# Windowed attention, a two-axis Fourier mix and an FFN on one core: pieces for GpSimd, a work order without the shared-port clock, and attention scores as 64x64 products by parity of the head

## The chip, the core and the metric

The kernel runs on one core of a Trainium2 chip. A core has TensorE (PE in the profile; its weight loads are PEld), VectorE (DVE), ScalarE (ACT), GpSimd (POOL) and SyncE (SP), which here issues nearly all DMAs. Each engine works through its own queue in order, and they meet only at semaphores. The metric is the device time of one execution in microseconds (us), lower is better.

## The reference

Inputs are q, k, v of shape (8, 8, 576, 64) (batch, heads, positions, head size) and two FFN weights, 512x2048 and 2048x512, which reach the kernel as 64-bit floats.

```
scores = q @ k.T / 8, kept where 0 <= row - col < 64, softmax over col
attn   = softmax @ v                     -> x (8, 576, 512), heads side by side
X      = real(fft over positions(fft over features (x)))
u      = x + X
un     = (u - mean) / sqrt(var + 1e-6)
out    = u + relu(un @ w_ch1) @ w_ch2
```

## The kernel before

The 8 x 576 positions of all batches form 36 tiles T of 128 positions; two batches (a pair) fill 9 tiles. Because the window is 64 wide, a block of 64 queries needs only its own 64 keys and the 64 before them.

**Two ways through a tile.** Tiles T < PRO = 13 are "whole": they stay in float32. q and k are turned on TensorE (`flip`, L464), copied out of PSUM, multiplied, masked and maximized on VectorE (`masked`, L587), exponentiated on ScalarE (`expo`, L595), turned again on TensorE (`flip_p`, L606), copied, and multiplied with v (`av`, L657). Tiles from 13 on are "split": each value becomes a high and a low float16 part. The low parts (`k_lo` L484, `q_part` L495, `p_lo` L620, `u_lo` L1045, `y_lo`) are subtractions on GpSimd or VectorE, and the turns are DMA transposes issued by SP (`k_turn` L487, `q_turn` L499, `p_turn` L626, `y_turn` L765, `u_turn` L1050).

**Scores.** jj counts the two blocks of 64 queries in a tile. One PSUM bank and one `pr` buffer hold block jj, with two heads on the two halves of the partitions. In a whole tile `q_copy` writes q block-diagonally into `qbd32` (the rest was set to zero once, L370), by two copies of 64 partitions, so one 128x128 product (L568) gives two heads; four such products make one block. In a split tile (L575) the two heads go to the two column halves of the array.

**After the attention.** `radix4` (L691) does the first butterflies of the feature transform into y, y is turned and kept as yT, and when a batch is complete `fft` does the rest (folds L804 and L806, sums L830 to L858, products L890 and L924). `norm_tile` gathers the mixed rows, adds, normalizes (`rs` on GpSimd, L1022; `scale`, L1026) and turns the result into `uhl`, the FFN's input, 256 positions at a time. `ffn(c)` runs 16 steps of a first product (`ph`, L1207), a relu into two parts (`hh`, ScalarE L1222 and VectorE L1225) and a second product (`po`, L1188), in three float16 passes; the first of the 18 chunks is float32 (PLAIN = 1). The weights arrive in 32 blocks of 512 KB (`weight_piece`), and VectorE makes float32 of each in three steps (L1099, L1104, L1111) into `w0s`, `w1s` and, for the last block of the first weight, `wf`.

**The order.** Every step is an operation of the planner `Plan` with an engine (or two to choose from), a duration, a priority and its buffers. `Plan.order` simulates the engines and writes each engine's queue in the order that the simulation finds. FFN products have the lowest priority, so they fill what is left of TensorE. The simulation has one more clock, `port`: a GpSimd step, and a VectorE step marked `port`, may start only when the last such step of either engine has ended. Steps that read PSUM are marked `port=False`. Where the simulation has a gap on TensorE before the FFN begins, products of a constant (`warm`, L1286) fill it.

Of the kernel before, what the change touches and what calls it, by code (L numbers as in the profile page):

```python
# [39 lines left out]
TURN = 1.26  # L40
HTURN = 1.2
# [8 lines left out]
PLAIN = 1  # L50
W_DMA, W_DMA_STEP, W_CONV, W_SQ, W_SPLIT, W_STEP = -20, 1.6, 40, 60, 60, 0.5
# [19 lines left out]
def _constants():  # L71
# [31 lines left out]
    sq = (np.arange(P) % 64)[:, None]  # L103
    t = np.arange(64)[None]
    own, old, none = t <= sq, t > sq, t + 0 * sq < 0
    mask = np.concatenate([np.where(m, 0.0, NEG) for m in (own, old, own, none, own)], axis=1)
# [23 lines left out]
class Plan:  # L130
# [65 lines left out]
    def order(self):  # L196
# [20 lines left out]
        port = 0.0  # L217
        res = []
        n = len(self.ops)
        while len(res) < n:  # L220
            best = None
            for e in engs:
                t0 = free[e]
                pick, ahead = None, []
                for o in avail[e]:
# [12 lines left out]
                    st = max(t0, r, port) if e == "POOL" or e == "DVE" and o.port else max(t0, r)  # L238
                    if len(o.durs) > 1:
                        (e1, d1), (e2, d2) = o.durs.items()  # L240
                        s1, s2 = (max(port, r) if x == "POOL" or x == "DVE" and o.port else r for x in (e1, e2))
                        sooner = max(free[e2], s2) + d2 + o.margin < max(free[e1], s1) + d1
                        if e != (e2 if sooner else e1):
                            continue
# [26 lines left out]
            if o.eng == "POOL" or o.eng == "DVE" and o.port:  # L271
                port = end
# [25 lines left out]
def attn_fft_ffn_kernel(ctx: ExitStack, tc: tile.TileContext, q, k, v, w1, w2, gidx, dft_d, dft_s, mask, out):  # L298
# [26 lines left out]
    mskb = cp.tile([P, 320], BF16, name="mskb")  # L325
# [5 lines left out]
    qbd32 = [b_.rearrange("p (a j h s) -> p a j h s", a=4, j=2, h=2) for b_ in qbuf]  # L331
# [37 lines left out]
    for i in range(2):  # L369
        op("POOL", 1.0, -498 + i, lambda i=i: nc.gpsimd.memset(qbuf[i], 0.0), writes=[Bq[i]])  # L370
# [30 lines left out]
    def copy(eng, out, in_, scale=None):  # L401
        if eng is nc.scalar:
            nc.scalar.mul(out, in_, scale) if scale is not None else nc.scalar.copy(out, in_)  # L403
        elif scale is not None:
            eng.tensor_scalar(out=out, in0=in_, scalar1=scale, scalar2=None, op0=ALU.mult)
        else:
            eng.tensor_copy(out, in_)

    xts, Bx, yTs, ByT, ByL, uhls, Bu, mds, Bmd = ({} for _ in range(9))

    def attn_tile(T, base):
# [34 lines left out]
        def keys(h, jj):  # L446


            if jj or n == 0:
                return kst_[:, h]  # L450
# [4 lines left out]
            return halves[:, own : old + (1 if step > 0 else -1) : step]  # L455

        if whole:
# [8 lines left out]
            def q_copy(h, eng):  # L466
                src = t["pq"][64 * h : 64 * h + 64].rearrange("p a (j s) -> p a j s", j=2)
                copy(eng, qbd32[i][64 * h : 64 * h + 64, :, :, h, :], src)

# [3 lines left out]
            for h in range(2):  # L473
                op("ACT", 0.48, base + 0.6, lambda e, h=h: q_copy(h, e), [bpq], [Bq[i]], alt=("DVE", 0.6), port=False)
        else:
# [13 lines left out]
            def q_part(z, eng):  # L489
# [4 lines left out]
                else:  # L494
                    eng.tensor_tensor(out=lo, in0=src, in1=hi, op=ALU.subtract)  # L495
# [6 lines left out]
            op("POOL", 1.12, base + 0.1, k_lo, [bk], [bkp], alt=("DVE", 0.6, lazy))  # L502
            op("DMA", TURN, base + 0.2, k_turn, [bkp], [bkT], lat=2.0)
            op("ACT", 0.95, base + 0.5, lambda e: q_part(0, e), [bq], Bfl[4:6], alt=("DVE", 0.6, lazy))
            op("POOL", 2.1, base + 0.6, lambda e: q_part(1, e), [bq], Bfl[4:6], alt=("DVE", 1.13, lazy))
# [50 lines left out]
        bpt = [None, None]  # L556
        for jj in range(2):
            J = 2 * n + jj
            m = ((192 if jj else 128) if J % 9 == 0 else (64 if jj else 0))
            bs, bp, bnm, bpp, bt = Buf("ps"), Buf("pr"), Buf(), Buf("ps"), Buf("pt")  # L560
            bpt[jj] = [bt]

            def score(jj=jj):
                t["pr", jj] = sb([P, 4, P], F32, "pr", f"pr{T}_{jj}")
                p_ = t["ps", jj] = bank("ps", f"psc{T}_{jj}")
# [5 lines left out]
                for hp in range(0 if whole else 4):  # L571
                    for z in range(2):
                        for x in range(2):
                            h = 2 * hp + x
                            nc.tensor.matmul(  # L575
                                p_[64 * x : 64 * x + 64, hp], qbd[i][:, jj, h, 64 * z : 64 * z + 64], keys(h, jj),
                                start=(z == 0), stop=(z == 1),
                            )

            rd = [Bq[i], bkT, *([] if jj or n == 0 else [BkT[before]])]  # L580
            op("PE", 0.95 if whole else 0.52, base + 2 + jj, score, rd, [bs, bp])

            def masked(jj=jj, m=m):

                t["nm", jj] = sm.tile([P, 4], F32, tag="nm", name=f"nm{T}_{jj}")
                for hp in range(4):
                    nc.vector.tensor_tensor_reduce(  # L587
                        out=t["pr", jj][:, hp], in0=t["ps", jj][:, hp], in1=mskb[:, m : m + P], scale=-0.125, scalar=3.0e38,
                        op0=ALU.add, op1=ALU.min, accum_out=t["nm", jj][:, hp : hp + 1],
                    )  # L590

            def expo(jj=jj):
                for hp in range(4):
                    pr = t["pr", jj][:, hp]
                    nc.scalar.activation(pr, pr, AF.Exp, bias=t["nm", jj][:, hp : hp + 1], scale=-1.0)  # L595
# [722 lines left out]
```

## Time and profile before

| | |
|---|---|
| median of 3 runs | 1019.76 us (1015.79, 1019.76, 1021.48) |
| profiled execution: first to last instruction | 1015.3 us |
| TensorE busy | 972.7 us, 96% |
| VectorE busy | 679.6 us, 67% |
| ScalarE busy | 417.9 us, 41% |
| GpSimd busy | 197.4 us, 19% |
| mean granted TensorE clock | 0.993 |

The profiled execution is known by its span of 1015.3 us; what lies around it is at most the difference to a run: 0.5 us to the fastest of the three and 4.5 us to their median. A line such as "L657 PE MATMUL pa<-va,pt 128*64 128x65 f32" names the line of the kernel, the engine, the operation, the tiles written and read, the rows and columns of the array that are used, and partitions by elements of what is moved. Float32 products stand as two records each. In a timeline the first number is the start, the second the duration, and brackets hold idle time before the instruction and what ended it.

### The profile page before, as it was taken

To read this page: it belongs to the slowest core of one execution; us is meant where nothing else is said; L and a number is where in the kernel's file an instruction comes from. 1 tells how busy PE (TensorE), PEld (TensorE's weight loads), DVE (VectorE), ACT (ScalarE), POOL (GpSimd) and SP (SyncE) were. 2 spreads that over 40 slices of the span, in tenths; PEclk is the share of its full clock that TensorE was granted. 3 is DMA by queue.
4 is the path that set the end of the run, shared out by engine and by line. 5 is a ranking of instruction groups with operands and counts; after the bars stand their busy time and mean duration, and the time that the engine had idled before them with its cause. 6 is when DMAs were issued, how large, how long until landed. Compare 5 with 4: busy or idle time off the path is not lost.

```text
span 1015.3 us, 22449 instructions
## 1 busy us (share of the span) xinstructions
PE 972.7 (96%) x8756; PEld 687.3 (68%) x8756; DVE 679.6 (67%) x1979; ACT 417.9 (41%) x1047; POOL 197.4 (19%) x203
## 2 busy tenths in 40 slices
PE   8889989999999989998999999999999999999998
PEld 7677757676676657665676666766676667676665
DVE  5899899888777767565787769676686636441121
ACT  6666656744554335323354335333453213121111
POOL 1000100042244223332022302233021300220000
PEclk9999999999999999999999999999999999999999
DMA  8987673235989866878668766867565421230000
GB/s 194 244 224 198 191 188 109 71 78 94 160 152 178 160 114 143 142 137 141 126 111 172 144 126 108 173 131 161 89 111 108 94 38 37 60 74 21 1 22 21
DMA packets 310538, 123.06 MB, mean 121 GB/s; under 512 B 292568, under 2 KB 292696, under 8 KB 310432
## 3 DMA queue, kind: packets, MB, share of 16 engines
q1 hardware_dynamic: 307712, 112.71, 54.8%
q0 software_dynamic: 2720, 8.92, 3.3%
q8 instruction: 69, 1.13, 0.5%
q14 instruction: 37, 0.30, 0.1%
HBM read 54.97 MB, written 14.17 MB: 68 GB/s over the span
## 4 chain that ended last, share of the span: by engine, by line
PE 75%; DVE 8%; DMA 8%; SPq 5%; ACT 2%; issue 2%; POOL 0%; DVEq 0%; ACTq 0%; POOLq 0%
PE ph L1207 30%; PE po L1188 30%; PE pz L924 3%; PE pa L657 3%; DMA pt<-flex 2%; DMA kn<-in_k 2%; PE pg L890 2%; PE psc L568 2%; PE psc L575 2%; SPq L626 2%; SPq L499 1%; DVE y L691 1%; PE pp L606 1%; SPq L427 1%; DVE pr L587 1%
## 5 line engine op out<-in xcount | busy, mean ns | idle before, releaser
L1207 PE MATMUL ph<-uhl,w0s 128*128 128x256 f16 (+1 forms) x3384 | 427.1, 277 | 10.1 <-DVE hh L1225 10.1
L1188 PE MATMUL po<-w1s,hh 128*128 128x512 f16 (+1 forms) x1696 | 428.1, 389 | 0.0
L1207 PEld LDWEIGHTS <-w0s 128*128 128x128 f16 x3264 | 318.0, 98 | 97.6 <-issue 14.5
L1225 DVE SCALAR_TENSOR_TENSOR hh<-ph,hh 128x256 f16<-128x256 f32 x272 | 114.5, 422 | 231.7 <-ACT hh L1222 225.8
L1222 ACT ACTIVATE hh<-ph 128x256 f16<-128x256 f32 x272 | 103.6, 382 | 392.9 <-PE ph L1207 297.1
L1188 PEld LDWEIGHTS <-hh 128*128 128x128 f16 x1632 | 157.0, 98 | 138.8 <-issue 1.9
L595 ACT ACTIVATE pr<-pr,nm 128x128 f32<-128x128 f32 x288 | 90.9, 392 | 13.2 <-DVE nm L587 13.1
L587 DVE CUSTOM_DVE_ANT_0 pr<-psc,mskb 128x128 f32<-128x128 f32 x288 | 65.5, 285 | 15.3 <-PE psc L568 11.3
L1045 POOL TENSOR_TENSOR up<-un,up 128x512 f16<-128x512 f32 x33 | 39.7, 1204 | 75.8 <-ACT up L403 73.1
L620 POOL TENSOR_TENSOR flex<-pr,flex 128x512 f16<-128x512 f32 x23 | 27.4, 1190 | 133.8 <-ACT flex L403 93.5
L1022 POOL TENSOR_TENSOR rs<-mv,mhalf 128x1 f32<-128x1 f32 x36 | 21.0, 584 | 157.9 <-DVE mv L1018 152.2
L484 POOL TENSOR_TENSOR flex<-kn,flex 128x512 f16<-128x512 f32 x19 | 25.0, 1314 | 125.0 <-ACT flex L403 119.3
L998 POOL DMA_INDIRECT mt<-md,gix x34 | 36.5, 1073 | 57.4 <-DMA md<-mp 48.8
L657 PE MATMUL pa<-va,pt 128*64 128x65 f16 (+1 forms) x760 | 39.3, 205 | 7.5 <-DMA pt<-flex 7.5
L657 PE MATMUL pa<-ve,pt 128*64 128x65 f16 (+1 forms) x760 | 39.4, 205 | 0.3 <-DMA ve<-va 0.3
L403 ACT CAST flex<-pr 128x512 f16<-128x512 f32 x39 | 24.0, 615 | 23.5 <-DMA pt<-flex 21.1
L691 DVE TENSOR_TENSOR y<-xu 128x256 f32<-128x256 f32 x68 | 32.1, 512 | 0.6
L669 DVE TENSOR_TENSOR xu<-pa,rc 128x256 f32<-128x256 f32 x72 | 30.6, 425 | 2.6
L568 PE MATMUL psc<-kst,qbd 128*128 128x128 f32 x208 | 28.2, 282 | 3.1 <-ACT qbd L403 1.2
L924 PE MATMUL pz<-g,ds__75 97*96 97x257 f16 (+3 forms) x240 | 29.3, 273 | 1.4 <-DVE g L900 1.4
L657 PEld LDWEIGHTS <-pt 128*64 128x64 f16 x1104 | 20.7, 113 | 14.7 <-DMA pt<-flex 7.9
L495 POOL TENSOR_TENSOR flex<-qn,flex 128x1024 f16<-128x1024 f32 x12 | 26.2, 2187 | 16.3 <-ACT flex L403 14.1
(155 smaller groups left out, 1108.0 us busy)
## 6 DMA issues: line engine op xcount, KB each, us to landing
wd<-in_moe_w_ch SPq DMA_DIRECT2D x20, 512.0 KB
out<-xu SPq DMA_DIRECT2D x36, 256.0 KB
ve<-va SPq DMA_DIRECT2D x67, 130.0 KB
kn<-in_k SPq DMA_DIRECT2D x32, 256.0 KB
qn<-in_q SPq DMA_DIRECT2D x32, 256.0 KB
flex<-in_moe_w_ch SPq DMA_DIRECT2D x12, 512.0 KB
flex<-in_v SPq DMA_DIRECT2D x20, 256.0 KB
md<-mp SPq DMA_DIRECT2D x24, 192.0 KB
```

The costliest lines, as they stand in the source:

```text
L568: nc.tensor.matmul(p_[:, hp], qw, keys(hp, jj), start=True, stop=True)
L587: nc.vector.tensor_tensor_reduce(out=t["pr", jj][:, hp], in0=t["ps", jj][:, hp], in1=mskb[:, m : m + P], scale=-0.125, scalar=3.0e38, op0= ...
L595: nc.scalar.activation(pr, pr, AF.Exp, bias=t["nm", jj][:, hp : hp + 1], scale=-1.0)
L657: nc.tensor.matmul(pa[64 * jj : 64 * jj + 64, hh], pt[:, sl], v_, start=(x == 0), stop=(x == len(mm) - 1))
L691: eng.tensor_tensor(out=o, in0=p0, in1=p1, op=al)
L924: nc.tensor.matmul(pz[:M, c0:c1], ds_[:NJ, a, c[0] : c[0] + c[1]], t["g", gi][:, b_, c0:c1], start=(x == 0), stop=(x == len(mm) - 1),)
L998: nc.gpsimd.indirect_dma_start(out=mts[T], out_offset=None, in_=mds[pb][0 : HR if n < 4 else 2 * HR], in_offset=bass.IndirectOffsetOnAxis( ...
L1045: eng.tensor_tensor(out=t["up"][:, 1], in0=t["un"], in1=t["up"][:, 0], op=ALU.subtract)
L1188: nc.tensor.matmul(t["po"][i], l_, r_, start=(f == 0 and x == 0), stop=(f == NKF - 1 and x == len(mm) - 1))
L1207: nc.tensor.matmul(ph, l_, r_, start=(x == 0), stop=(x == len(mm) - 1))
L1222: nc.scalar.activation(t["hh", f][:, 0], ph, AF.Relu)
L1225: nc.vector.scalar_tensor_tensor(out=hh[:, 1], in0=ph, scalar=0.0, in1=hh[:, 0], op0=ALU.max, op1=ALU.subtract)
```

## The change

Four things change together.

- **Pieces.** A helper `both` splits a GpSimd two-operand step into 4 (8 for `q_part`) instructions along the second axis; on VectorE the step stays one. The planner's GpSimd durations rise (1.12 to 1.4, 2.1 to 2.8, 2.35 to 2.6, 0.95 to 1.2).
- **Order.** The clock `port` leaves the simulation, so GpSimd and VectorE steps may be planned side by side.
- **Scores by parity.** A PSUM bank and a `pr` buffer now hold the four heads of parity g, with the two query blocks jj on the two partition halves. In a whole tile q is copied plainly by one copy of 128 partitions, nothing is zeroed, and 16 products of 64 rows, 64 columns and 128 moved columns take the four quarters of the array in turn: rows by g, columns by jj. They are one planner step of 1.6 (before: two of 0.95) that takes two PSUM banks at once. Split tiles keep their products with the roles of head and block exchanged. `av` of parity g waits for the turned weights of g alone, and the mask is one 128-wide table per tile.
- **Transposes.** `p_turn` becomes one DMA transpose of 128 partitions per g instead of two of 64; the planner's duration of a transpose is 1.5 everywhere (before 1.26, and 1.2 for the half ones).

```diff
-TURN = 1.26
-HTURN = 1.2
+TURN = 1.5
+WSC = 1.6
...
-                    st = max(t0, r, port) if e == "POOL" or e == "DVE" and o.port else max(t0, r)
+                    st = max(t0, r)
...
-            if o.eng == "POOL" or o.eng == "DVE" and o.port:
-                port = end
...
+    def both(eng, out, in0, in1, al, n=4):
+        w = out.shape[1] // n if eng is nc.gpsimd else out.shape[1]
+        for k in range(0, out.shape[1], w):
+            eng.tensor_tensor(out=out[:, k : k + w], in0=in0[:, k : k + w], in1=in1[:, k : k + w], op=al)
...
-            for h in range(2):
-                op("ACT", 0.48, base + 0.6, lambda e, h=h: q_copy(h, e), [bpq], [Bq[i]], alt=("DVE", 0.6), port=False)
+            op("ACT", 0.48, base + 0.6, lambda e: copy(e, q32[i], t["pq"]), [bpq], [Bq[i]], alt=("DVE", 0.6), port=False)
...
-                eng.tensor_tensor(out=kp[:, :, 1], in0=t["kn"], in1=kp[:, :, 0], op=ALU.subtract)
+                both(eng, kp[:, :, 1], t["kn"], kp[:, :, 0], ALU.subtract)
...
-                for hp in range(4 if whole else 0):
-                    qw = qbd32[i][:, hp, jj].rearrange("p h s -> p (h s)")
-                    nc.tensor.matmul(p_[:, hp], qw, keys(hp, jj), start=True, stop=True)
+        def score(groups):
+            for g in groups:
+                t["pr", g] = sb([P, 4, P], F32, "pr", f"pr{T}_{g}")
+                t["ps", g] = bank("ps", f"psc{T}_{g}")
+            for hp in range(4):
+                for z in range(1 if whole else 2):
+                    for g in groups:
+                        for jj in range(2):
+                            out = t["ps", g][64 * jj : 64 * jj + 64, hp]
+                            if whole:
+                                rows = slice(64 * g, 64 * g + 64)
+                                nc.tensor.matmul(
+                                    out, q32[i][rows, hp, 64 * jj : 64 * jj + 64], keys(hp, jj, rows), start=True, stop=True
+                                )
...
-            op("DMA", HTURN, base + 4.2 + jj, lambda g=p_turn: g(0), [bpp], [bt, bt2], lat=1.8)
-            op("DMA", HTURN, base + 4.3 + jj, lambda g=p_turn: g(1), [bpp], [bt2], lat=1.8)
+            op("POOL", 1.4, base + 4.1 + g, p_lo, [bp], [bpp], alt=("DVE", 0.6, lazy))
+            op("DMA", TURN, base + 4.2 + g, p_turn, [bpp], [bt], lat=2.2)
...
-            rd = [*bpt[0], *bpt[1], Bve[i], Bva[i]]
+            rd = [*bpt[g], Bve[i], Bva[i]]
```

## Rows read from the trace of the kernel before

**Rows 1.** The page: the span, and busy time of each engine.
```profile
span 1015.3 us, 22449 instructions
PE 972.7 (96%) x8756; PEld 687.3 (68%) x8756; DVE 679.6 (67%) x1979; ACT 417.9 (41%) x1047; POOL 197.4 (19%) x203
```

**Rows 2.** Busy time by stretch: the stretch, its length, busy us (instructions) of each engine, the granted clock, the mean busy share of the DMA engines, GB/s.
```profile
0.00:86.00 86.00, 73.28 (x716) 59.73 (x717) 68.18 (x259) 55.16 (x143) 7.13 (x20) 0.98 0.90 222
86.00:146.00 60.00, 59.23 (x362) 43.21 (x360) 54.06 (x152) 36.90 (x98) 4.92 (x5) 1.00 0.71 189
146.00:160.00 14.00, 9.92 (x68) 7.27 (x67) 13.09 (x39) 4.33 (x11) 0.72 (x1) 0.88 0.57 142
160.00:230.00 70.00, 68.24 (x545) 49.72 (x542) 62.23 (x158) 44.64 (x100) 13.73 (x15) 1.00 0.29 81
230.00:820.00 590.00, 570.54 (x5665) 396.72 (x5664) 416.89 (x1227) 241.32 (x605) 156.19 (x146) 0.99 0.72 133
820.00:1015.00 195.00, 191.48 (x1414) 130.69 (x1411) 65.16 (x151) 35.58 (x92) 14.70 (x16) 1.00 0.13 33
```

**Rows 3.** Who TensorE waited for, the longest sums: total us, times, longest.
```profile
PE ph L1207 <- DVE hh L1225: 10.1, 10, 2.8
PE pa L657 <- DMA pt<-flex: 7.5, 4, 3.8
PE ph L1207 <- DVE wf L1111: 3.7, 1, 3.7
```

**Rows 4.** Timeline of TensorE in a whole tile: scores (8 records for a block of 64 queries), and products with v on alternating column halves.
```profile
76.03 1.06 PE L568 MATMUL psc<-kst,qbd 128*128 128x128 f32 x8
77.02 0.63 PE L464 MATMUL pq<-ident,qn 128*128 128x128 f32 x4
...
79.21 0.27 PE L657 MATMUL pa<-ve,pt 128*64 128x65 f32 x1
...
79.32 0.22 PE L657 MATMUL pa<-ve,pt 128*64 128x65 f32 x1
...
79.38 0.22 PE L657 MATMUL pa<-ve,pt 128*64 128x65 f32 x1
79.38 0.22 PE L657 MATMUL pa<-va,pt 128*64 128x65 f32 x1
```

**Rows 5.** The same stretches as rows 2 for the whole tiles' scores (L568) alone: busy us (records) of PE and PEld, clock, DMA share, GB/s.
```profile
0.00:86.00 86.00, 17.65 (x134) 16.01 (x135) 0.98 0.90 222
86.00:146.00 60.00, 7.16 (x52) 6.12 (x50) 1.00 0.71 189
...
160.00:230.00 70.00, 3.37 (x24) 2.99 (x24) 1.00 0.29 81
```

**Rows 6.** The chain of waits from 0 to 90 us: its shares by line (of 90 us), and two of its pieces with start and length.
```profile
by line: DMA kn<-in_k 15.7%; PE psc L568 13.2%; PE mt L967 5.7%; PE pp L606 5.7%; PE pa L657 5.3%; PE pk L464 5.1%; PE warm L1286 4.9%; PE pq L464 4.7%; ACT qbd L403 4.4%; PE ph L1207 4.1%; PE pz L924 3.7%; issue 3.0%; DVE pr L587 1.8%; ACT
...
38.53 6.08 DMA kn<-in_k
...
47.42 0.58 ACT qbd L403
...
48.02 0.58 ACT qbd L403
```

**Rows 7.** The chain of waits from 140 to 158 us: the two loads of weight blocks in it.
```profile
137.62 5.28 DMA flex<-in_moe_w_ch
...
148.03 4.49 DMA wd<-in_moe_w_ch
```

**Rows 8.** SP's issue time of a transpose of the softmax weights (64 partitions): min, median, max in ns.
```profile
L626 SPq DMA_TRANSPOSE pt<-flex x92: 1193/1264/2272, 254.4 to 820.9; - x92
```

**Rows 9.** SP's issue time of a transpose of k (128 partitions, as many columns).
```profile
L487 SPq DMA_TRANSPOSE kst<-flex x23: 1231/1316/2780, 156.3 to 735.2; - x23
```

**Rows 10.** Timeline of TensorE in a split tile: the longest wait for the turned weights.
```profile
365.85 0.26 PE L657 MATMUL pa<-va,pt 128*64 128x65 f16 x1 [3.76 <-DMA pt<-flex]
```

**Rows 11.** Timeline of GpSimd: one `q_part`.
```profile
280.86 2.12 POOL L495 TENSOR_TENSOR flex<-qn,flex 128x1024 f16<-128x1024 f32 x1
```

**Rows 12.** Timeline of VectorE: the same step twice, the second beside the GpSimd instruction of rows 11.
```profile
279.95 0.56 DVE L858 TENSOR_TENSOR hs<-h,hs 128x388 f16<-128x388 f32 x1
...
282.02 1.38 DVE L858 TENSOR_TENSOR hs<-h,hs 128x388 f16<-128x388 f32 x1
```

**Rows 13.** The butterflies of `radix4` (L691) on VectorE and on GpSimd: min, median, max in ns, first and last start.
```profile
L691 DVE TENSOR_TENSOR y<-xu x68: 408/419/1390, 17.1 to 830.3; 128x256 f32<-128x256 f32 x68
L691 DVE TENSOR_TENSOR y<-y x68: 278/291/2207, 17.8 to 830.9; 128x128 f32<-128x128 f32 x68
...
L691 POOL TENSOR_TENSOR y<-y x4: 449/454/459, 695.9 to 753.4; 128x128 f32<-128x128 f32 x4
```

**Rows 14.** The page's costliest groups on GpSimd: count, busy us, mean ns, idle time before.
```profile
L1045 POOL TENSOR_TENSOR up<-un,up 128x512 f16<-128x512 f32 x33 | 39.7, 1204 | 75.8 <-ACT up L403 73.1
L620 POOL TENSOR_TENSOR flex<-pr,flex 128x512 f16<-128x512 f32 x23 | 27.4, 1190 | 133.8 <-ACT flex L403 93.5
...
L484 POOL TENSOR_TENSOR flex<-kn,flex 128x512 f16<-128x512 f32 x19 | 25.0, 1314 | 125.0 <-ACT flex L403 119.3
...
L495 POOL TENSOR_TENSOR flex<-qn,flex 128x1024 f16<-128x1024 f32 x12 | 26.2, 2187 | 16.3 <-ACT flex L403 14.1
```

**Rows 15.** VectorE's relu part (L1225): min, median, max in ns.
```profile
L1225 DVE SCALAR_TENSOR_TENSOR hh<-ph,hh x272: 408/424/427, 172.1 to 1006.8; 128x256 f16<-128x256 f32 x136
```

More of the change, by code (lines that the diff above doesn't have):

```diff
@@ L99, in _constants @@
     )
-    sq = (np.arange(P) % 64)[:, None]
+    sq = np.arange(64)[:, None]
     t = np.arange(64)[None]
     own, old, none = t <= sq, t > sq, t + 0 * sq < 0
-    mask = np.concatenate([np.where(m, 0.0, NEG) for m in (own, old, own, none, own)], axis=1)
+    first, second = (own, old), (old, own)
+    both = [(first, second), ((own, none), second), (first, (none, own))]
+    mask = np.where(np.concatenate([np.block([list(a), list(b)]) for a, b in both], axis=1), 0.0, NEG)
     g = np.arange(2 * S)
@@ L324, in attn_fft_ffn_kernel @@
     mhalf = cp.tile([P, 1], F32, name="mhalf")
-    mskb = cp.tile([P, 320], BF16, name="mskb")
+    mskb = cp.tile([P, 3 * P], BF16, name="mskb")
     unit = cp.tile([P, P], F32, name="unit")
@@ L444, in attn_tile, with keys @@
         kst_ = (kst32 if whole else kst16)[:, T % 3 * kw : (T % 3 + 1) * kw].rearrange("p (h s) -> p h s", s=P)
-        def keys(h, jj):
+        def keys(h, jj, rows=slice(None)):
             if jj or n == 0:
-                return kst_[:, h]
+                return kst_[rows, h]
             halves = (kst32 if whole else kst16).rearrange("p (x s) -> p x s", s=64)
@@ L454, in keys @@
             step = old - own
-            return halves[:, own : old + (1 if step > 0 else -1) : step]
+            return halves[rows, own : old + (1 if step > 0 else -1) : step]
         if whole:
@@ new lines, in attn_tile @@
+        bpt, bss = [], [Buf("ps"), Buf("ps")]
+        m = P * (1 if n == 0 else 2 if n == 4 else 0)
+        rd = [Bq[i], bkT, *([] if n == 0 else [BkT[before]])]
+        def score(groups):
[12 more added lines that the diff above has]
+                                )
+                            else:
+                                h = 2 * hp + g
+                                nc.tensor.matmul(
+                                    out, qbd[i][:, jj, h, 64 * z : 64 * z + 64], keys(h, jj), start=(z == 0), stop=(z == 1)
+                                )
@@ L586, in masked @@
+        bps = [Buf("pr"), Buf("pr")]
+        if whole:
+            op("PE", WSC, base + 2, lambda: score((0, 1)), rd, [*bss, *bps])
+        for g in range(2):
+            bs, bp, bnm, bpp, bt = bss[g], bps[g], Buf(), Buf("ps"), Buf("pt")
+            bpt.append([bt])
+            if not whole:
+                op("PE", 0.52, base + 2 + g, lambda g=g: score((g,)), rd, [bs, bp])
+            def masked(g=g):
+                t["nm", g] = sm.tile([P, 4], F32, tag="nm", name=f"nm{T}_{g}")
                 for hp in range(4):
@@ L717, in keep @@
                     else:
-                        eng.tensor_tensor(out=dst, in0=src[:, 0], in1=src[:, 1], op=ALU.add)
+                        both(eng, dst, src[:, 0], src[:, 1], ALU.add, 4 if m > 1 else 1)
             if lo == S * bb and n > 0:
@@ L829, in first @@
                 t[nm, which] = sb([P, 4, NJ], F32, "r3", f"{nm}{which}_{b}")
-                eng.tensor_tensor(out=t[nm, which], in0=up, in1=dn, op=al)
+                both(eng, t[nm, which], up, dn, al)
             def mid(nm=nm, src=src):
@@ L838, in tot @@
             def tot(eng, nm=nm, src=src):
[L839 removed]
+                both(eng, t[nm, 0], t[nm, 0], view(src)[0], ALU.add)
             pr = base + 1 + x
[L842 removed]
+            two = {"alt": ("POOL", 1.2, lazy)}
             op("DVE", 0.47, pr, lambda e, f=first, w=o_sum: f(e, w, ALU.add), [b1], [b3[o_sum]], **two)
```

152 lines of the change are left out of this document (57 added, 95 removed).

## The prediction

> **What bounds the kernel now.** I read the page first, then busy time by stretch, then TensorE's waits, then the chain of waits at the two places where TensorE stands still. On the page TensorE is busy for 972.7 of 1015.3 us [rows 1], so 42.6 us are all that better timing alone could return; more has to come out of TensorE's own work. The stretches say where the idle time is [rows 2]: 12.7 us of the first 86, before the FFN has input; 4.1 of the 14 from 146 on; 19.5 of the 590 from 230 to 820, where split tiles and the FFN share the engine; 3.5 after 820, where only FFN is left. The granted clock is 0.98 to 1.00 of its upper level, 2.4 GHz, except from 146 to 160, where it reads 0.88 around a standstill. The waits name the causes [rows 3]: 10.1 us for the relu parts `hh`, 7.5 for the turned softmax weights, 3.7 once for the last weight block `wf`. So the kernel is a TensorE queue with FFN as filler, which loses time where a step in its fixed order is not ready when the engine reaches it. A change helps by shortening TensorE's work or by making those steps ready; relief of another engine counts only as far as it does that.
>
> **Scores of the whole tiles.** Eight records take 0.99 us from start to start [rows 4], 0.124 us a record, so a tile's 16 take 2.0 us. The new form has 16 products, 32 records, each still moving 128 columns. The trace has no product on a row half, so I bound it. None side by side: 32 x 0.124 = 4.0 us. Column halves alone side by side: 2.0. All four quarters: 1.0. The nearest row is the product with v: its pairs on alternate column halves start every 0.06 us [rows 4], 0.03 a record, where 65 of 128 columns at 0.124 would be 0.063; the column halves do run side by side. The row halves differ from them in reading different partitions and in writing different banks, which leaves nothing that they share and the column halves don't. I take four, and add 0.2 us for the array's change of form on the way in and out, because the first pair on column halves takes 0.11 us where later ones take 0.06 [rows 4]: 1.2 us, and 1.3 with a first product that finds the array empty. Saved: 0.7 us a tile; bounds +0.8 and, with the halves in series, -2.2.
>
> The Trainium skill (TensorEngine Tiling (Array Packing), Key Properties) says that the tiles of the array work independently and that a change of tiling mode drains the engine. By that rule the tile would cost 1.0 us plus two drains, which the 0.11 against 0.06 fits; no run so far shows the row halves.
>
> Where does it count? After 160 us stand 24 of the records [rows 5], 1.5 tiles: **-1.0 us**. From 86 to 146 stand 52, 3.25 tiles: 2.3 us. Before 86 TensorE isn't full, and only the chain counts.
>
> **The start.** In the chain of the first 90 us the scores hold 13.2%, 11.9 us, and the q copies 4.4%, 4.0 us [rows 6]. The second copy of each pair (0.58 us each [rows 6]) goes: -2.0. The scores shrink by a third: -4. But the chain also holds 14.1 us of loads of k, the longest of 6.08 us ending at 44.6 [rows 6], at a DMA share of 0.90 [rows 2]; what is won ahead of a load waits at it. I count 2.5 of the 6. With the 2.3 above, 4.8 us are won ahead of 146 us.
>
> There TensorE stands 3.7 us for `wf` [rows 3], whose block comes late since the last loads are issued only when VectorE has emptied a buffer [rows 7]; VectorE is busy for 54.1 of the 60 us before [rows 2]. If the blocks come no earlier, all 4.8 us are lost in a longer standstill. VectorE does get relief: it loses a few q copies, and without the shared clock the planner can give butterflies to GpSimd, busy for 4.9 of these 60 us. A tile's butterflies are two of 419 and two of 291 ns on VectorE [rows 13], 1.4 us. But most of what VectorE does here has two operands in SBUF, and waits while GpSimd reads (next part), so little of it is net. I take half: **-2.4 us** (0 to -4.8).
>
> **Transposes.** On SP a transpose of 64 partitions takes 1.264 us [rows 8] and one of 128 partitions and as many columns 1.316 [rows 9]: the count costs, not the partitions. Four become two, 5.06 - 2.63 = 2.4 us a tile of SP's queue, 56 us over 23 split tiles; behind them stand the transposes of q, k, y and u and the loads. `av` also no longer waits for the other parity. The waits this addresses are the 7.5 us [rows 3], in four pieces of which one is 3.76 [rows 10]. The landing time stays, so I take 60%: **-4.5 us** (0 to -7.5). What is late next is `hh`.
>
> **Pieces and the order.** A GpSimd step of 512 columns takes 1.19 to 1.31 us on the mean, one of 1024 2.19 [rows 14]; a piece of 128 takes 0.454 [rows 13]. Four are 1.8 us and eight 3.6, somewhat less where they overlap: up to 0.6 and 1.4 us later for the low parts, behind which stand their transposes on SP. The chunk that comes out is needed much later: after 820 us TensorE lives for 195 us on what lies ready [rows 2]. For k and q it adds to a tile's latency, which FFN work covers if the planner knows of it; it plans 1.4 and 2.8, so up to 0.4 and 0.8 us are not planned. That cover ends where the step comes sooner than planned, and then it costs TensorE that difference.
>
> The gain and the danger are at the shared access to SBUF. A VectorE step of 0.56 us took 1.38 beside a `q_part` that ended at 282.98 [rows 11, 12]; a butterfly of 291 ns took up to 2207 [rows 13]. `hh` itself isn't stretched, 424 ns at the median and 427 at most [rows 15], but it stands in VectorE's queue behind steps that are, and TensorE waits 10.1 us for it [rows 3]. Pieces cut one hold from 2.1 us to about 0.45; the missing clock makes holds many more. Bounds: -5 (half of the 10.1) and +19 (third rival). I take **0**.
>
> **Sum.** -1.0 - 2.4 - 4.5 + 0 = -7.9: a span of 1007.4 us. The median of the runs is 4.5 us over the span of the profiled execution, which I keep: **1012 us**, 0.8% faster. Its own range is 1004 to 1018.
>
> **Rivals.**
>
> *More is returned.* The blocks of weights come earlier with the rest, the waits for turned weights go altogether, and shorter holds halve the waits for `hh`: 1.0 + 4.8 + 7.5 + 5 = 18.3, 1001 us at the median; with 3 us more off the start, 998. For it: GpSimd is nearly idle before 230 us while VectorE is busy for eight to nine tenths [rows 2]. Against it: every GpSimd step that reads SBUF holds up VectorE's two-operand steps.
>
> *It doesn't do what it says.* The row halves don't run side by side: with 2.0 + 0.2 us a tile the scores lose 0.2 x 4.75 = 1 us after 86, the standstill at 146 eats what the q copies win, and of the 4.5 us at the transposes the late k and q low parts take 2: 1019.8 + 1 - 2.5 = 1018 us. For it: no row shows row halves. Against it: the column halves [rows 4].
>
> *Collisions.* The four groups of rows 14 hold GpSimd for 118 us; in pieces, at 1.8 against 1.2, 175. If a third of that meets a two-operand step of VectorE, VectorE loses 58 us, in `hh`'s queue, and if a third of this reaches TensorE, 19 us: 1012 + 19 = 1031 us. It decides from about 8 us on, where it has eaten the gain. For it: collisions exist already, with a clock made against them [rows 12, 13], and a queue written from a simulation that doesn't know of them is wrong wherever they happen. Against it: VectorE has 29% of its time free from 230 to 820 [rows 2], and TensorE's lateness gives everyone slack.
>
> The Trainium skill (SBUF — State Buffer, Who interferes with whom) says that GpSimd and a VectorE step with two SBUF inputs exclude each other for the whole instruction, and speaks for this rival; the trace agrees (1.38 us against 0.56). [...]
>
> **Chances.** Forecast 0.43, more returned 0.17, does not do what it says 0.22, collisions 0.18. A measurement of this kernel can tell about 0.5% from no change, 5 us: 1014.7 to 1024.9. Faster gets four fifths of the forecast (0.34), the first rival, and a quarter of the second (0.05): 0.56. Slower gets the third rival and a rest of 0.01. The range of 996 to 1030 takes in the first rival's 998 and nearly the third's 1031, and leaves out their far halves, 0.17 together.
>
> **What would show it.** In the changed kernel's trace: 32 records of 64 rows for a tile's scores within about 1.2 us (2 would make the second rival right); one copy of q a tile; TensorE's wait for `wf` no longer than 3.7 us and sooner than 146; two transposes `pt` a split tile, and waits of `pa` for them of about 3 us instead of 7.5; waits for `hh` near 10. The prediction is wrong if the waits for `hh` and `y` double, or if the stretch of split tiles grows.

## The result and the profile after

The changed kernel takes 1024.22 us at the median (1020.36 to 1026.97, 12 runs), the kernel before 1019.94 on the same chip: a ratio of 1.0054, 95% interval 1.0030 to 1.0077. It got slower by some 5 us. I had forecast 1012 us and gave "slower" 0.19; the time lies in my range of 996 to 1030, on the side of the third rival.

The page after, span and busy time [rows 1]:

```profile
span 1020.3 us, 23272 instructions
PE 976.6 (96%) x9032; PEld 681.2 (67%) x9032; DVE 679.0 (67%) x1979; ACT 407.7 (40%) x1032; POOL 294.7 (29%) x542
```

Only GpSimd has changed much: 294.7 us for 197.4. The same stretches as [rows 2], same columns:

```profile
0.00:86.00 86.00, 69.34 (x862) 54.05 (x863) 62.46 (x240) 48.56 (x127) 12.57 (x30) 0.96 0.87 218
86.00:146.00 60.00, 53.34 (x347) 38.22 (x344) 54.27 (x134) 28.85 (x80) 12.39 (x17) 0.91 0.66 186
146.00:160.00 14.00, 12.67 (x87) 8.65 (x86) 11.37 (x33) 8.14 (x23) 7.30 (x16) 1.00 0.21 57
160.00:230.00 70.00, 68.44 (x556) 48.02 (x556) 60.77 (x151) 42.47 (x96) 21.61 (x35) 1.00 0.37 96
230.00:820.00 590.00, 576.88 (x5770) 399.02 (x5768) 422.18 (x1272) 243.30 (x614) 225.89 (x422) 1.00 0.66 135
820.00:1015.00 195.00, 194.85 (x1416) 132.95 (x1415) 66.51 (x151) 36.42 (x94) 14.99 (x22) 1.00 0.11 28
```

Against the kernel before, the loss stands in the first two rows: TensorE is busy for 122.7 of the first 146 us (132.5 before), and from 86 to 146 the granted clock is 0.91 of the upper level where it was 1.00. More of that busy time is filler, too. These are the products of a constant, before and after, all of them ahead of 146 us (count; busy us, mean ns; idle before):

```profile
L1286 PE MATMUL warm<-ident 128*128 128x256 f16 x80 | 14.0, 314 | 1.3 <-POOL ident masks.py:199 1.3
...
L1279 PE MATMUL warm<-ident 128*128 128x256 f16 x148 | 23.0, 305 | 1.4 <-POOL ident masks.py:199 1.4
```

Some comes back later: from 160 to 820 us TensorE is busy for 645.3 us, 638.8 before. TensorE's waits [rows 3]: total, times, longest:

```profile
PE ph L1200 <- DVE hh L1218: 9.2, 11, 2.5
PE py L743 <- DVE y L409: 7.2, 4, 3.9
PE pu L1031 <- DVE xu L662: 5.7, 1, 5.7
...
PE pa L652 <- DMA pt<-flex: 1.2, 1, 1.2
```

The wait for the turned weights is nearly gone (1.2 for 7.5), and the one for `wf` has no row left. The waits for `hh` stay at 9.2. Those for `y` have grown to 7.2 (before 2.7), 5.0 of it in the first 150 us, and one of 5.7 in the start is new. TensorE's timeline shows that one, and a whole tile's scores:

```profile
48.55 1.10 PE L568 MATMUL psc<-kst,qbd 64*64 64x128 f32 x32
...
83.56 5.96 PE L1279 MATMUL warm<-ident 128*128 128x256 f16 x53
95.26 1.08 PE L1031 MATMUL pu<-ident,un 128*128 128x128 f32 x4 [5.74 <-DVE xu L662]
...
100.57 1.06 PE L1200 MATMUL ph<-uhl,w0s 128*128 128x256 f32 x2
```

The 32 records take 1.10 us: all four quarters work side by side. But the first FFN product comes at 100.57 us; in the kernel before it came at 86.25:

```profile
86.25 1.46 PE L1207 MATMUL ph<-uhl,w0s 128*128 128x256 f32 x6
```

And GpSimd by line and form (count; busy us, mean ns; idle before) [rows 13, 14]:

```profile
L409 POOL TENSOR_TENSOR flex<-qn,flex 128x128 f16<-128x128 f32 x128 | 63.4, 530 | 61.6 <-DVE flex L403 24.9 <-ACT flex L399 22.6 <-DVE y L409 7.4
L409 POOL TENSOR_TENSOR flex<-pr,flex 128x128 f16<-128x128 f32 x96 | 51.6, 567 | 118.1 <-ACT flex L399 109.5 <-DVE flex L403 5.1 <-issue 2.2
...
L409 POOL TENSOR_TENSOR flex<-kn,flex 128x128 f16<-128x128 f32 x52 | 29.3, 592 | 19.0 <-DVE va L527 7.9 <-ACT flex L399 7.6 <-DVE flex L403 2.3
...
L409 POOL TENSOR_TENSOR f<-xe 128x97 f32<-128x97 f32 x28 | 17.3, 651 | 88.9 <-DVE xe L409 88.9
L409 POOL TENSOR_TENSOR h<-yT 128x97 f32<-128x97 f32 x28 | 14.5, 551 | 5.0 <-DVE fs L409 3.8 <-DVE rc L658 1.2
```

A piece of 128 columns, 415 ns at its quickest in this trace, takes 530 to 592 ns on the mean in the three costliest groups: now GpSimd stands in front of the shared access. And it does FFT steps (`f`, `h`, `hs`) that VectorE did before, all but one. To follow this through the runs I use one sum of my own, the *excess*: over all instructions of one engine that overlap one of the other, the time above the quickest quartile of the same line, tiles and form (for GpSimd, above the quickest). Before: VectorE 31 us, GpSimd 12. After: 23 and 69.

One place of TensorE's longest wait for `hh`, in the chain of waits from 380 to 388 us:

```profile
380.07 0.73 POOL f L409 x3
...
381.42 0.78 DVE f L827
...
382.22 0.67 DVE f L409
382.89 0.34 DVE hh L1218
383.23 1.88 DVE fs L409 x3
385.10 1.41 DVE h L409 x2
386.51 0.35 DVE hh L1218
...
386.90 1.14 PE ph L1200 x9
```

GpSimd's four `f` pieces, behind its own low halves of `pr`, make VectorE wait 2.02 us until 381.42; what VectorE still has to do then (0.66 us a step on the mean, where rows 12 has 0.56 for a step of that width) stands in front of `hh`, and TensorE, which waits 2.51 us, starts at 386.90.

### The profile page after: what moved, and what is told of

It reads as the page before. It is cut to its first block, busy times and chain, and to the rows that moved or that the text cites. A ratio compares the mean times of both kernels' runs of the same rounds, so it can differ in the third digit from the quotient of the medians.

```text
span 1020.3 us, 23272 instructions
## 1 busy us (share of the span) xinstructions
PE 976.6 (96%) x9032; PEld 681.2 (67%) x9032; DVE 679.0 (67%) x1979; ACT 407.7 (40%) x1032; POOL 294.7 (29%) x542
## 4 chain that ended last, share of the span: by engine, by line
PE 55%; DVE 6%; DMA 5%; POOL 4%; issue 2%; ACT 1%; SPq 0%; DVEq 0%; ACTq 0%; POOLq 0%
PE ph L1200 25%; PE po L1181 24%; POOL flex L409 2%; PE pz L917 2%; PE pg L883 2%; PE pa L652 1%; DMA py<-yp 1%; DMA mt<-md,gix 1%; DMA uhl<-up 1%; PE psc L573 1%; DMA kn<-in_k 1%; DVE hh L1218 1%; DVE y L409 1%; DMA pt<-flex 0%; DVE h L409 0%
## 5 line engine op out<-in xcount | busy, mean ns | idle before, releaser
L409 POOL TENSOR_TENSOR flex<-pr,flex 128x128 f16<-128x128 f32 x96 | 51.6, 567 | 118.1 <-ACT flex L399 109.5
L409 POOL TENSOR_TENSOR flex<-qn,flex 128x128 f16<-128x128 f32 x128 | 63.4, 530 | 61.6 <-DVE flex L403 24.9
L652 PE MATMUL pa<-ve,pt 128*64 128x65 f16 (+1 forms) x760 | 42.9, 205 | 1.6 <-DMA pt<-flex 1.2
L409 POOL TENSOR_TENSOR f<-xe 128x97 f32<-128x97 f32 x28 | 17.3, 651 | 88.9 <-DVE xe L409 88.9
L652 PE MATMUL pa<-va,pt 128*64 128x65 f16 (+1 forms) x760 | 42.9, 205 | 0.0
L409 POOL TENSOR_TENSOR flex<-kn,flex 128x128 f16<-128x128 f32 x52 | 29.3, 592 | 19.0 <-DVE va L527 7.9
L662 DVE TENSOR_TENSOR xu<-pa,rc 128x256 f32<-128x256 f32 x72 | 30.5, 424 | 2.5
L399 ACT CAST up<-un 128x512 f16<-128x512 f32 x31 | 19.1, 616 | 28.1 <-DMA uhl<-up 13.0
L399 ACT CAST flex<-pr 128x512 f16<-128x512 f32 x39 | 24.0, 616 | 13.6 <-DMA pt<-flex 13.3
L573 PEld LDWEIGHTS <-qbd 128*64 128x64 f16 x736 | 22.0, 110 | 11.0 <-issue 10.9
```

The costliest lines, as they stand in the source:

```text
L409: eng.tensor_tensor(out=out[:, k : k + w], in0=in0[:, k : k + w], in1=in1[:, k : k + w], op=al)
L573: nc.tensor.matmul(out, qbd[i][:, jj, h, 64 * z : 64 * z + 64], keys(h, jj), start=(z == 0), stop=(z == 1))
L652: nc.tensor.matmul(pa[sl, hp], pt[:, sl], v_, start=(x == 0), stop=(x == len(mm) - 1))
```

## The experiments

All are against the kernel before, each ratio with its 95% interval. Two things are kept apart: runs in which the **written order** of steps is that of the run they are compared with, and runs in which the edit also makes the planner write another order. Four results lay well outside all that I had written down ahead: e7 and e9 came out faster, e10 and e18 slower.

**The start: e1.** The new score step is planned at 1.1 us.

```diff
-WSC = 1.6
+WSC = 1.1
```

> The changed kernel with one number altered: the planner's duration of a whole tile's score step is 1.1 us, near what its trace shows (32 records in 1.10), instead of 1.6. The instructions are the same, only the order differs. Theory A (the loss is made at the start: the score step of a later tile takes two of the four PSUM banks at once, the softmax product takes the other two, VectorE converts weights before it empties them, and the turn of the first normalized tile waits for a bank): with another order the four banks are not all taken there, the FFN starts near 86 to 90 us instead of 100.6, and the time is 1008 to 1016 us. Theory B (collisions at the shared access to SBUF, everywhere, since the planner no longer knows of them): they stay, and the time is 1020 to 1028 us.

1.0069 (1.0044 to 1.0095). The FFN begins at 90.7 us instead of 100.6, and the kernel is no faster: the waits for `hh` rise to 17.8 us. So an order with an earlier FFN can lose as much elsewhere. Since it is another order, e1 doesn't show what the late FFN costs in after.

**The clock: e2, e3, e8.** The clock `port` is taken from the kernel before (e2; its main line below), put back into the one after (e3), or put back only where the engine is chosen (e8).

```diff
-                    st = max(t0, r, port) if e == "POOL" or e == "DVE" and o.port else max(t0, r)
+                    st = max(t0, r)
...
```

> The kernel before, with the clock of the shared port taken out of the planner and nothing else changed. Theory A: the clock's absence does no harm by itself, 1012 to 1022 us, and the FFN starts no later than 88 us. Theory B: GpSimd and VectorE meet more often, whole steps of 1.2 and 2.1 us block each other, waits for hh and y double, 1030 to 1040 us.

> The changed kernel with the planner's clock of the shared port put back, all else as changed. Theory B: faster than the changed kernel, 1010 to 1016 us, with fewer stretched VectorE steps. Theory A: the clock only reshuffles the start; if the FFN still starts late or the clock makes TensorE wait in the split tiles, 1018 to 1030 us.

> The kernel after with the common clock put back only where the engine of a step is chosen, not where the start of a step is set. If the loss comes from the number of steps put on GpSimd, this is as e3: 0.991 to 0.996, GpSimd's instructions near e3's. If it comes from the order, which lets steps of the two engines overlap, this is as the kernel after: 1.003 to 1.008, with VectorE's excess near 23 us and GpSimd's near 69.

e2: 1.0193 (1.0147 to 1.0239), VectorE's excess 56 us. e3: 0.9931 (0.9902 to 0.9960), excess 12 and 29. e8: 1.0061 (1.0040 to 1.0082), as after. So the clock is worth 20 us on the old kernel (17 between the medians) and 12 on the new one, and a clock in the choice of engine alone brings nothing: what acts is that start times respect it, for e8 differs from e3 in that alone. Each of these edits also writes another order, so the sizes hold an order's luck; the sign is the same in two more pairs below (e7 and e10, e13 and e18). One thing missed: e8's excess is 20 and 39 us, not the 23 and 69 of after that I expected with its time, so the excess doesn't measure the loss. In e3 the waits for `hh` fall to 2.9 us:

```profile
PE ph L1204 <- DVE hh L1222: 2.9, 5, 1.4
```

**Pieces: e4, e5, e13.** GpSimd's steps whole again, with order and planned durations kept: in the kernel after (e4) and in e3 (e5). e13 puts pieces into e9 (below), again in the old order.

```diff
-        w = out.shape[1] // n if eng is nc.gpsimd else out.shape[1]
+        w = out.shape[1]
```

> The changed kernel with its GpSimd steps whole again, in the same order with the same planned durations: only the pieces go. Theory A: the start has few GpSimd steps, so the FFN starts at 100 us as before; between 230 and 820 us the waits grow by a few us because one hold lasts 1.2 to 2.1 us: 1022 to 1032 us. A rival C (pieces cost more than they return, as each piece pays its own overhead and can be held up by itself): 1014 to 1020 us.

> The kernel after with the common clock of GpSimd and of VectorE's shared-port steps put back (as in e3), and with GpSimd's steps whole again. The order and the choice of engine are e3's. If the pieces win by themselves, as they did without the clock (e4 to after, about 7 us), this loses about 7 us on e3: a ratio near 1.000 against the kernel before. If the pieces only heal what the missing clock opens, there is little left to heal: within 2 us of e3, 0.991 to 0.995, and if each piece's own start costs more than it frees, slightly below e3. VectorE's excess over its undisturbed durations should rise from 12 us towards the 31 us of the kernel before, and GpSimd's fall from 29 to 12.

> e9 (the kernel before with one transpose for two in the old order) with GpSimd's steps in pieces, and the order, the engines and the planned durations all kept. Theory: the pieces win by themselves, as in e5 to e3 and e4 to after, 5 to 7 us: 0.976 to 0.979, VectorE's excess falling from 33 to about 15 us and GpSimd's rising. Rival: with the transposes no longer late, the held-up VectorE steps have room and pieces are worth nothing: 0.982 to 0.985. Second rival: the longer steps of GpSimd (some 1.55 us for 1.12) make the transposes late again: 0.987 or above, with a wait of PE for the transposed probabilities.

e4: 1.0122 (1.0094 to 1.0151). e5: 0.9980 (0.9962 to 0.9998). e13: 0.9801 (0.9762 to 0.9841), 997.93 us. In one and the same order the pieces win 7, 5 and 3 us; the intervals of the second pair just miss each other, those of the third overlap, and its 3 us are not clear of noise. Each time they move the stall from VectorE to GpSimd: excess from 54 and 24 (e4) to 23 and 69 (after), from 33 and 11 (e9) to 21 and 36 (e13).

**Transposes: e6, e9, e15.** The kernel before with one transpose of 128 rows for two of 64. In e6 it is one planned step of 1.26 us. In e9 the two steps stay in the plan, and the first issues nothing, so every other step keeps its place. e15 is e6 with a later planned landing (3.4 for 2.2 us).

```diff
-                nc.sync.dma_start_transpose(dst, t["pp", jj][64 * h : 64 * h + 64].rearrange("p a z t -> p (a z t)"))
+                nc.sync.dma_start_transpose(dst, t["pp", jj].rearrange("p a z t -> p (a z t)"))
...
+            op("DMA", HTURN, base + 4.2 + jj, lambda: None, [bpp], [bt, bt2], lat=1.8)
+            op("DMA", HTURN, base + 4.3 + jj, lambda g=p_turn: g(), [bpp], [bt2], lat=1.8)
```

> The kernel before with one edit: the two 64-row transposes of each score chunk become one of 128 rows, with the same data, the same duration in the written order as the other transposes, and nothing else of the change. My prediction put this part at -4.5 us, that is 0.9956. Rival one: all of e3's 7 us come from here, 0.993 or less. Rival two: SyncE's queue was covered and the whole gain of e3 lies in the scores and in the order by parity: 0.999 to 1.001. PE's wait for the transposed probabilities should fall from 7.5 us to 1 to 3 us in the first two cases.

> As e6, but the order of every other step is kept exactly as in the kernel before: of the two planned 64-row transposes the first issues nothing, and the second issues the one of 128 rows in its place. Theory: the transposes are worth a few us by themselves and e6's +5 us came from the other order that the planner wrote for them: 0.995 to 0.999, PE's wait for the transposed probabilities well under 7.5 us. Rival: SyncE was covered, and one transpose of 128 rows comes no earlier than the second of two: 0.999 to 1.001. Second rival: the larger transpose itself costs (it is there later than the first half was): 1.003 or above, as e6.

> e6 with one number changed: the plan takes a transpose of the probabilities to land 1.2 us later than e6's plan did (3.4 us after its issue instead of 2.2), about as late as e9's plan has it. The instructions are e6's and e9's. If e6 lost because its order counts on transposes that come later than planned, this is near e9, 0.983 to 0.989, and PE's waits for the hidden layer's VectorE step fall from 8 us to 3 to 5. If orders simply differ by chance, it can lie anywhere between 0.983 and 1.005.

e6: 1.0048 (1.0026 to 1.0070). e9: **0.9833** (0.9808 to 0.9859). e15: 1.0026 (0.9994 to 1.0059). The same instructions in another order are 22 us apart, and a plan with more slack doesn't explain it. What the transposes do by themselves shows in the view of their own line, who waited for it, before and then in e9:

```profile
L626 SPq DMA_TRANSPOSE pt<-flex x92: 1193/1264/2272, 254.4 to 820.9; - x92
...
who waited for it (us, times):
  ACT flex L403: 21.1, 17
  PEld L657: 7.9, 4
  PE pa L657: 7.5, 4
  DVE flex L407: 6.7, 5
```

```profile
L625 SPq DMA_TRANSPOSE pt<-flex x46: 1232/1317/2838, 257.8 to 803.7; - x46
...
  ACT flex L403: 7.7, 9
  DVE flex L407: 4.0, 4
  PEld L657: 0.7, 2
  PE pa L657: 0.3, 1
```

I had read only TensorE's 7.5 us. ScalarE waited 21.1 us: the transposes read the buffer `flex` into which it writes the next tile's high halves, and in its queue stands the relu's first part. In e9 it waits 7.7, and TensorE's wait for `hh` falls too, from 10.1:

```profile
PE ph L1207 <- DVE hh L1225: 3.0, 7, 0.7
```

**The same on two other orders: e11 and e14, e12 and e16.** e11 is e7 (below) with two transposes of 64 rows; e14 keeps e11's plan with one. e12 is the kernel before with only the planned durations of the one after; e16 keeps e12's plan with one transpose.

```diff
-TURN = 1.26
+TURN = 1.5
...
-            op("POOL", 1.12, base + 0.1, k_lo, [bk], [bkp], alt=("DVE", 0.6, lazy))
+            op("POOL", 1.4, base + 0.1, k_lo, [bk], [bkp], alt=("DVE", 0.6, lazy))
...
```

> e7 with each transpose of the probabilities cut into two of 64 rows, as in the kernel before (now one for each chunk of queries), and the products reading them so. My prediction gave the merging 4.5 us: then this is 0.988. If, as e6 has it, merging costs or is worth nothing, this is 0.979 to 0.984.

> e11's order and plan, in which the first of each pair of transposes issues nothing and the second transposes all 128 rows. If one transpose for two is worth some 17 us in any order, this is 0.977 to 0.981. If it is worth what e7 won on e11, 0.983 to 0.985. If e9 was a lucky case, 0.990 to 0.994.

> The kernel before with nothing but the planned durations of the kernel after: 1.5 us for a transpose, 1.2 to 2.8 us for GpSimd's steps. The instructions are the same, the written order and some choices of engine differ. This measures what a mere reordering does. If orders are alike in worth, 0.998 to 1.002. If a reordering by itself moves the time by several us, as I suspect from e6, it falls outside, to either side, and then no single part of the change under 5 us can be read off two kernels with different orders. Part of the gain of e3 (7 us) may also be in these durations: then 0.993 to 0.997, with GpSimd's busy time below 197 us.

> e12's order and plan with one transpose for two. Worth some 17 us in any order: 0.978 to 0.983. Worth only the pt wait that e12 shows (2.6 us against 7.5 before): 0.993 to 0.996, since e12 had fewer late transposes.

e11: 0.9943 (0.9920 to 0.9967), e14: 0.9887 (0.9849 to 0.9925): 5.7 us. e12: 0.9970 (0.9946 to 0.9993), e16: 0.9927 (0.9901 to 0.9952): 4.4 us. So the merging wins in each of three orders, 17, 6 and 4 us, the last two with intervals that overlap. What goes with the size are TensorE's waits for `hh` and `pt` together: 17.6 us before and 3.3 in e9, but 10.1 in e12 and 6.5 in e16, whose rows are these:

```profile
PE ph L1207 <- DVE hh L1225: 7.5, 10, 2.5
PE pa L657 <- DMA pt<-flex: 2.6, 4, 0.9
...
PE ph L1207 <- DVE hh L1225: 5.4, 8, 2.5
PE pa L657 <- DMA pt<-flex: 1.1, 1, 1.1
```

ScalarE's wait is not the price. From e12 to e16 it falls nearly as far as in e9, from 19.1 to 8.3 us, for a gain of 4 us, and in e6, which has 46 transposes as well, it stands at 19.7. That e9's gain is the largest because the order of the kernel before waited most is argued from these waits. e12 also shows that a reordering alone moves this kernel by some 3 us.

**The joint score step: e7, e10.** The whole tile's scores as two steps, one for each parity and bank: with the clock (e7, against e3) and without (e10, against after).

```diff
-            op("PE", WSC, base + 2, lambda: score((0, 1)), rd, [*bss, *bps])
+            pass
...
-            if not whole:
-                op("PE", 0.52, base + 2 + g, lambda g=g: score((g,)), rd, [bs, bp])
+            if True:
+                op("PE", WSC / 2 if whole else 0.52, base + 2 + g, lambda g=g: score((g,)), rd, [bs, bp])
```

> e3 with the whole tile's score step cut in two, one for each parity, each with one bank; two quarters of the array side by side instead of four. Theory: the joint step takes two of the four banks at once and keeps them while their readers wait, which costs the start some 4 us; cutting it gives those back and costs at most 0.7 us a whole tile on TensorE, of which the tiles ahead of the FFN are half covered. Net -3 to +2 us on e3, 0.990 to 0.995, with the first step of the FFN at 86 to 88 us instead of 90.7. Rival: four quarters side by side are what e3's gain is made of, then this goes back to 0.998 or above, and the score records of a whole tile take 2 us in all again.

> The kernel after with the whole tile's score step cut in two, one for each parity, and nothing else: still no common clock. Between e3 and e7 this edit gave about 10 us. Theory: it gives the same here, since what it frees are the banks ahead of 100 us and nothing of the clock: 0.994 to 0.998, and the first step of the FFN comes near 86 us. Rival: without the clock the start's gain is taken back later by collisions, as in e1: 1.003 to 1.008.

e7: 0.9836 (0.9809 to 0.9863), 10 us better than e3. e10: 1.0132 (1.0108 to 1.0157), 8 us worse than after, though its FFN begins at 85.2 us. The edit does a second thing: a step of one parity has only two quarters of the array side by side. Its 16 records take as long as the joint step's 32 (1.10), so the scores of the 13 whole tiles take TensorE 27.6 us in e7 and 14.4 in e3. Here one in e10:

```profile
84.19 1.09 PE L568 MATMUL psc<-kst,qbd 64*64 64x128 f32 x16 [0.76 <-ACT uhl L399]
```

The signs differ, and both runs have orders of their own, so what the joint step is worth stays open. What isn't open is the sign of the clock, which lies between e7 and e10: 30 us.

**What is left: e17, e18.** In e17 GpSimd writes zeros where it would compute low halves, in after's order. e18 is e13 without the clock.

```diff
+        if lo and eng is nc.gpsimd:
+            return eng.memset(out, 0.0)
```

> The kernel after in its own order, but wherever GpSimd would compute the low half of keys, queries, probabilities or normalized rows, it writes zeros in one instruction: that part of the computation is left out, the time is all that is read. If the loss against e3 lies in these steps (held up and holding up VectorE), this wins at least the 12 us that lie between e3 and after: 0.985 to 0.994. If it lies in the order as such, whatever GpSimd does in it, it stays above 1.000. In between, the rest is with GpSimd's FFT, radix and gather steps, which are kept.

> e13 (old layout of the scores, one transpose for two, pieces) with the common clock of GpSimd and VectorE's shared-port steps taken out, as in the change. The clock's removal cost 17 us before (e2), 12 us in e3 to after and 30 us in e7 to e10. If it costs 12 to 30 here too: 0.992 to 1.010, with VectorE's excess above e13's. If pieces make the clock needless where the transposes are on time and the scores keep one bank a step: 0.978 to 0.985.

e17: 0.9953 (0.9935 to 0.9971). 10 us go with the low halves' work, in one and the same order; neither the 12 that I asked for nor nothing. The rest of the distance to e3 (0.9931) is within the intervals. The FFN begins at 99.8 us here, as late as in after, and the kernel is still faster than the one before. Writing zeros is also shorter (570 ns on the mean for the 512 columns of `up`, where four pieces take 4 x 458 ns), so this doesn't part the collisions from GpSimd's being late. e18: 1.0277 (1.0250 to 1.0304): the clock's removal costs some 50 us where the rest is best. TensorE's waits in e13 and then e18:

```profile
PE ph L1212 <- DVE hh L1230: 4.0, 7, 1.2
...
PE pa L662 <- DMA pt<-flex: 0.6, 1, 0.6
```

```profile
PE ph L1208 <- DVE hh L1226: 17.9, 19, 2.9
PE pa L658 <- DMA pt<-flex: 9.5, 7, 2.5
PE ph L1208 <- ACT hh L1223: 5.7, 2, 5.1
```

GpSimd's excess is 36 us in e13 and 74 in e18: steps that come late there turn up as late transposes and late `hh`. VectorE's waits for GpSimd's results go the same way in the pairs with pieces: 2.7 us in e3 and 13.3 in after, 1.0 in e7 and 14.4 in e10, 3.7 in e13 and 19.3 in e18. With whole steps it is another path: these waits are 2.5 us before and 1.9 in e2, and VectorE's own excess grows, from 31 to 56 us. e8 has neither (3.6 us, and an excess of 20), so for it the path stays open.

## Why the prediction was wrong

**Scores: right.** I took 1.2 us a whole tile; 1.10 was measured, 0.9 us saved where my upper bound was 0.8. The second rival (halves in series) falls; its 0.2 us lost a tile is the figure for it, and the bound of -2.2 that I put beside it belongs to products of which none run side by side. What the 1.0 us after 160 was worth can't be seen among changes of several us.

**The start: wrong in sign, and by stages this is where the time went.** I counted 4.8 us won and half kept, -2.4. The FFN begins 14.3 us later. The step "won ahead of 146 us" left out what the joint score step needs, two free banks at once; TensorE waits 5.74 us for `xu` (L662), after which a bank comes free, and from 91.6 to 101.9 us, with TensorE busy for 5.7 of these 10.3 us, the granted clock is 0.50, its lower level of 1.2 GHz. That the banks are the reason is argued from e10, where the step asks for one bank at a time and the FFN begins at 85.2 us. In the first 160 us TensorE is busy for 7.1 us less, and the products of the constant alone fill some 8 us more of that: some 15 us lost where I forecast 2.4 won. From 160 to 820 us it is busy for 6.5 us more, where I forecast waits shorter by 4.5, and its busy time without the constant is 4 us shorter (958.5 for 962.7); that makes the 5 us by which the profiled execution is longer. The start is no price by itself, though: e17, with the same order and the same late FFN, is 5 us faster than the kernel before, and with the clock back the FFN begins at 90.7 us (e3).

**Transposes: right in kind, too small.** "The waits this addresses are the 7.5 us" was the failing phrase: in e9 the waits for `hh` fell by 7.1 us along with them. The way there may lead through ScalarE, which the transposes held for 21.1 us through the buffer they read, but the runs don't show that. In the old order the part is worth 17 us; 6 and 4 in the others. My 4.5 is the lower end.

**Pieces and the order: "I take 0" is the step that failed.** It joined two edits of opposite sign. The pieces alone win 7 and 5 us in two orders; the 3 us in a third are not clear of noise. The clock's removal, with the order that it writes, costs 12 (e3 to after), 20 (before to e2), 30 (e7 to e10) and some 50 (e13 to e18). Part of that is the late start. The third rival had its kind (a queue written from a simulation that doesn't know of collisions) and its size at the low end (19 us), but not its place: I had VectorE losing 58 us beside GpSimd, while in pieces it is GpSimd that loses, 69 us of excess for 12, and in the runs with pieces TensorE's part comes by late GpSimd results that VectorE and SP wait for. Of the two waits that I had named as a sign of being wrong, `y`'s more than doubled and `hh`'s did not.

**Together**, along one path of runs, in us of the median before: one transpose for two, order kept, -17 (e9); pieces, order kept, -3 (e13); scores by parity in two steps, with another order, +4 (e7); the joint step, +10 (e3); the clock out, +12 (after): +6 of the +5.5 measured. The last three each have an order of their own and may not be read as prices. The gain that I forecast is there, and more; the clock's removal took it. That e3, the change with the clock left in, stands at 1012.13 us, just my forecast, is luck: its start, with the FFN at 90.7 us, lost where I counted a gain, and the rest won more than I counted.

Left open: whether the banks make the start late, by what path e8 loses, what makes e6's and e15's orders 22 and 20 us worse than e9's, and whether the layout by parity pays at all; its best run (e7, 0.9836) equals e9 without it. The fastest version found is e13, the kernel before with one transpose for two, pieces and its clock: 997.93 us, 0.9801 (0.9762 to 0.9841), not clear of e9 and e7.

## What to carry to other kernels

Where a planner writes the order, a part of a change is measured only with the order held (keep the planned steps, change what they issue); otherwise its order is measured with it, here up to 22 us. A shared resource stays in the planner's model even when each hold has been made short: without it the engine that yields changes, but its results are late all the same. A slow transfer can stand behind more of the bounding engine's waits than the one put down to it: look at all who wait for it, the writers of its source among them, and at what they hold up in turn. And where a queue is filled up with products of a constant, take them out before you read its busy time.

## What was not expected of the hardware

Cutting GpSimd's steps reverses who yields. Whole, VectorE's steps stretch (in e4 `un`, a step on 512 columns, takes 797 ns on the mean and 4058 at most, in after, in the same order, 580 and 975; the median is 545 in both) and GpSimd's do so less (24 us of excess, 69 in pieces). In pieces, a piece waits for the VectorE step that it finds running: of after's 360 pieces of 128 columns, 415 ns at the quickest, 109 take over 520 ns, and each of these ends 275 to 320 ns after a VectorE step that it overlapped, 96 of them after the one that was running when they began. Of the 77 pieces that began beside `pr` from `psc` or `xu` from `po` or `pa`, VectorE steps that read PSUM, none took over 439 ns. The Trainium skill (SBUF — State Buffer, Who interferes with whom) says that the order of issue decides who blocks; these 96 pieces agree, since the VectorE step was under way first. In e17, where GpSimd writes zeros, VectorE's butterflies with two operands are back at 430 and 290 ns, but `un`, with one, takes 708 (median 546, 2208 at most):

```profile
L1021 DVE TENSOR_SCALAR un<-xu,mv,rs 128x512 f32<-128x512 f32 x36 | 25.5, 708 | 3.4 <-POOL rs L1017 3.3
...
L411 DVE TENSOR_TENSOR y<-xu 128x256 f32<-128x256 f32 x64 | 24.9, 430 | 1.0
...
L411 DVE TENSOR_TENSOR y<-y 128x128 f32<-128x128 f32 x64 | 18.6, 290 | 1.1
```

I read this as: a GpSimd step that only writes lets the two-operand steps pass and still holds up some steps with one operand. No run had writes alone, so it isn't shown apart from GpSimd's other steps.
